# Gating steps ahead of evictions, a chunk's token sums behind the weights, transposes kept whole

## The chip, the cores and the metric

The kernel runs on one core of a Trainium2 chip. The metric is device time in microseconds (us), the median of several executions. Engines are called by the names of the profile: PE (TensorE matmul; PEld is its weight load), DVE (VectorE), ACT (ScalarE), POOL (GpSimd), SP (SyncE, which issues the DMAs).

## The reference

Three parts follow each other; all is float32.

```python
# 1 attention: a pooled branch (mean over groups of 4 positions) and a local one (|i-j| < 4), added
attn_out = out_up + out_local                      # (2, 8, 576, 64)
x = attn_out.transpose(0, 2, 1, 3).reshape(1152, 512)

# 2 mixture of experts over 1152 tokens, D = 512, 8 experts, F = 1024
P = np.exp(x @ w_gate - (x @ w_gate).max())
for _ in range(8):
    P /= P.sum(1, keepdims=True) + 1e-09
    P /= P.sum(0, keepdims=True) + 1e-09
    P *= N / E
for e in range(E):
    out += P[:, e:e + 1] * (np.maximum(x @ w1[e], 0.0) @ w2[e])

# 3 gated stage, F = 1536
return ((out @ w_a) * (out @ w_b)) @ w_out
```

## The kernel before, in words

**Numbers.** Every float32 operand of a large product is split into a rounded high part and a remainder (`xh`, `xl`; `w.hi`, `w.lo`; `gh`, `gl`; `Th`, `Tl`), and each product is three matmuls: high by high, high by low, low by high. A split is a cast on ACT (L132 for weights, L544 for token sums, L680 for transposed tiles) and a subtraction on DVE or POOL (L133, L545, L681).

**Units and chunks.** An expert is two units (halves of F). The 16 expert units are `units[0]` to `units[15]`, the gated stage has six, `glu_g[0]` to `glu_g[5]`. The 1152 tokens are in nine tiles of 128 and two chunks: chunk 0 (tiles 0, 1, 7, 8; 256 columns in each of its halves) and chunk 1 (tiles 2 to 6; 320 columns). The first two units are plain products. All later ones use a scheme with seven products in place of eight: the weights give the operands A11, S2, S1, A12, S3, A22, S4 (S1 to S4 are sums or differences of quarters, `comb`, L236, on POOL; S2, S1, S3 and S4 also have their low parts from POOL), and each takes its token operand from `xh`/`xl` or from the four sums T1 to T4 in `Th`/`Tl`. `g_chunk` issues the seven products of one unit and chunk in that order, each 12 matmuls, and behind each the additions into G tiles (L595) that free the PSUM banks. `phase` puts the second matmuls of the unit and chunk before between them (`o_tile`, one of 128 tokens, 12 matmuls of 512 columns; the results go to `acc` by L464, L466 or L470).

**Token sums.** `combine_x` makes T1 to T4 of one chunk as a list of tasks: four totals (`xh + xl`, L529, two on DVE and two on POOL, or as `tot` says), four differences (L537, DVE) and four splits (L544 on ACT, L545 on DVE or POOL as `low` says).

**What sets the order.** Engines run their instructions in the order in which the program issues them. Side work waits in queues: `wq` (weight preparation), `tq` (token sums), `dq` (decoding of later weights). `pump` runs tasks from them as a planner's clocks `M.pe`, `M.dve`, `M.pool` allow; `force` runs them until a weight that the next product needs is there, `tq` ahead of `wq`. `while tq: run(tq)` empties a queue at once.

**From gating to unit 2.** Once attention is done (`closed`), the gating is a generator that `step` advances by one piece after each product of the first two units (`g_plain`: 4 blocks of unit 1; then three `o_moe` tiles of the first unit): a reduction over experts on DVE, a matmul with ones on PE for the sum over tokens, a reduction and a scaling on DVE, eight times. Then come chunk 0's last sums, chunk 1's sums, and unit 2's products:

```python
        tq.extend(combine_x(1, lambda name: t1[name], (v, g, g, v), (g, g, g, g)))   # chunk 1's sums
        phase(units[2], 0, firsts[1])
```

**From the experts to the gated stage.** The gated stage needs the output transposed: `t_step(tt)` transposes a finished tile of `acc` on PE into a PSUM bank of the pool "o" (two banks, shared with `o_tile`), splits it from there into `xh` (ACT) and `xl` (DVE). The four tiles of chunk 0 are transposed beside the last unit's chunk 1, the five of chunk 1 after it, each one `o_tile` late; the token sums of chunk 0 are queued behind tile 8's step and emptied after three of the five, and the other two `o_tile`s with their steps stand inside `glu_g[0]`'s chunk 0, at places 0, 1 and 2 of its products.

## Time and profile before

| | |
|---|---|
| median of 3 runs | 1185.61 us (1177.13, 1185.61, 1187.04) |
| profiled execution | 1174.93 us, span 1173.2 us |
| mean granted clock of TensorE | 0.974 |
| busy, share of the span | PE 94%, PEld 84%, DVE 71%, ACT 39%, POOL 46% |
| DMA | 84.50 MB, mean 72 GB/s |

The profiled execution is the program run once under the hardware profiler; its span goes from the first to the last instruction. The clock is the mean share of TensorE's full speed that was granted while the program ran. An engine is busy while an instruction of it executes, and the shares are means over stages that differ.

### The profile page before, as it was taken

The numbers are of one execution on the slowest core, as the hardware profiler recorded it, in microseconds if no ns is written. First come the engines' busy times: TensorE is split into PE (matmuls) and PEld (weight loads), VectorE is DVE, ScalarE is ACT, GpSimd is POOL, SyncE is SP. The second block draws the span as 40 slices with busy tenths as digits, with TensorE's granted clock in tenths as the row PEclk, the third lists the DMA queues.
The fourth block names the chain that finished last, engine by engine and source line by source line (L and its number), as shares of the span: only waits on it lengthen the run. The fifth ranks groups of instructions, "written<-read, shape, count | busy, mean of one in ns | idle before, by whom it ended". The sixth has DMA issues, their size and how long they took to land.

```text
span 1173.2 us, 18031 instructions
## 1 busy us (share of the span) xinstructions
PE 1099.5 (94%) x6545; PEld 985.2 (84%) x6545; DVE 838.1 (71%) x1613; ACT 453.2 (39%) x1186; POOL 544.4 (46%) x537
## 2 busy tenths in 40 slices
PE   8898998369999999999999999999999869999998
PEld 6797887358888888988898889889899768999997
DVE  5666455636978898788887987888744677776764
ACT  5654341023444335344444344443443423323221
POOL 3413212333655645555546546554563545555431
PEclk9899999769999999999999999999999989999999
DMA  5342110003313232143232321322211101111102
GB/s 147 99 124 67 34 44 1 0 1 99 115 59 115 91 100 99 56 135 99 72 116 75 116 94 60 119 94 94 88 45 46 37 19 37 55 54 32 42 18 81
DMA packets 79720, 84.50 MB, mean 72 GB/s; under 512 B 34832, under 2 KB 53264, under 8 KB 79632
## 3 DMA queue, kind: packets, MB, share of 16 engines
q1 hardware_dynamic: 79632, 83.36, 22.9%
q8 instruction: 51, 0.84, 0.3%
q14 instruction: 37, 0.30, 0.1%
HBM read 71.54 MB, written 11.80 MB: 71 GB/s over the span
## 4 chain that ended last, share of the span: by engine, by line
PE 76%; DVE 12%; ACT 5%; POOL 3%; issue 2%; DMA 0%; DVEq 0%; SPq 0%; ACTq 0%; POOLq 0%
PE g L60 71%; PE at L60 3%; DVE w L133 3%; ACT w L132 1%; DVE acc L470 1%; DVE G L595 1%; ACT p L832 1%; POOL gl L591 1%; DVE xt L537 1%; ACT G L587 1%; ACT gh L589 1%; POOL p L847 1%; DMA kn<-in_k_dram 0%; DVE dec L338 0%; DVE dec L347 0%
## 5 line engine op out<-in xcount | busy, mean ns | idle before, releaser
L60 PE MATMUL g<-w,gh 128*128 128x512 f32 x1314 | 417.1, 398 | 11.7 <-DVE acc L470 8.1
L60 PE MATMUL g<-xh,w 128*128 128x256 f32 (+2 forms) x1472 | 329.0, 304 | 25.8 <-ACT w L132 23.1
L591 POOL TENSOR_TENSOR gl<-G,gh 128x256 fp32r<-128x256 f32 (+1 forms) x216 | 184.6, 863 | 298.9 <-ACT gh L589 277.3
L60 PEld LDWEIGHTS g<-w,gh 128*128 128x128 f32 x1314 | 237.6, 190 | 57.0 <-DVE acc L470 9.0
L60 PEld LDWEIGHTS g<-xh,w 128*128 128x128 f32 x1472 | 248.3, 190 | 31.9 <-ACT w L132 23.2
L60 PE MATMUL g<-w,gl 128*128 128x512 f32 x657 | 259.3, 395 | 0.0
L60 PE MATMUL g<-Th,w 128*128 128x256 f32 (+1 forms) x960 | 214.7, 300 | 14.4 <-ACT Th L544 4.8
L60 PE MATMUL g<-xl,w 128*128 128x256 f32 (+2 forms) x736 | 222.4, 302 | 0.8 <-POOL xl L905 0.5
L133 DVE TENSOR_TENSOR w<-raw,w 128x512 fp32r<-128x512 f32 x141 | 145.1, 1041 | 105.8 <-ACT w L132 105.8
L595 DVE TENSOR_TENSOR G<-g,G 128x256 f32<-128x256 f32 (+1 forms) x400 | 163.9, 449 | 38.7 <-PE g L60 26.7
L60 PEld LDWEIGHTS g<-Th,w 128*128 128x128 f32 x960 | 162.9, 191 | 21.0 <-ACT Th L544 5.1
L587 ACT ACTIVATE G<-G 128x256 f32<-128x256 f32 (+1 forms) x168 | 74.3, 443 | 244.0 <-DVE G L595 243.0
L60 PEld LDWEIGHTS g<-w,gl 128*128 128x128 f32 x657 | 124.4, 189 | 28.7
L60 PEld LDWEIGHTS g<-xl,w 128*128 128x128 f32 x736 | 139.8, 190 | 5.5 <-POOL xl L905 1.0
L60 PE MATMUL g<-Tl,w 128*128 128x256 f32 (+1 forms) x480 | 142.8, 298 | 0.2 <-DVE Tl L545 0.2
L589 ACT CAST gh<-G 128x256 fp32r<-128x256 f32 (+1 forms) x216 | 93.7, 434 | 109.6 <-DVE G L605 94.2
L132 ACT CAST w<-raw 128x512 fp32r<-128x512 f32 x181 | 107.5, 620 | 23.4 <-POOL raw L236 21.7
L470 DVE SCALAR_TENSOR_TENSOR acc<-g,P,acc 128x512 f32<-128x512 f32 x126 | 93.6, 743 | 23.3 <-PE g L60 22.5
L60 PEld LDWEIGHTS g<-Tl,w 128*128 128x128 f32 x480 | 91.8, 191 | 3.6 <-DVE Tl L545 0.6
L366 POOL TENSOR_TENSOR dec<-dec 128x384 f32<-128x384 f32 x48 | 50.8, 1057 | 77.5 <-DVE dec L363 56.4
L236 POOL TENSOR_TENSOR s<-raw 128x512 f32<-128x512 f32 x40 | 65.2, 1631 | 8.2 <-DMA raw<-in_moe_w_dram 6.7
L133 POOL TENSOR_TENSOR w<-s,w 128x512 fp32r<-128x512 f32 x40 | 59.0, 1474 | 13.9 <-ACT w L132 13.9
(156 smaller groups left out, 1211.9 us busy)
## 6 DMA issues: line engine op xcount, KB each, us to landing
raw<-in_moe_w_dram SPq DMA_DIRECT2D x64, 512.0 KB
w<-dec SPq DMA_DIRECT2D x48, 192.0 KB
dec<-in_moe_w_a_dram SPq DMA_DIRECT2D x16, 384.0 KB
dec<-in_moe_w_b_dram SPq DMA_DIRECT2D x16, 384.0 KB
dec<-in_moe_w_out_dram SPq DMA_DIRECT2D x16, 384.0 KB
raw<-w SPq DMA_DIRECT2D x48, 128.0 KB
raw<-w SPq DMA_DIRECT2D x6, 512.0 KB
vw<-in_v_dram SPq DMA_DIRECT2D x72, 35.0 KB
```

What stands on the lines that cost most here:

```text
L60: nc.tensor.matmul(out=o, lhsT=l, rhs=r, start=start, stop=stop, skip_group_check=not check)
L132: nc.scalar.copy(out=hi, in_=raw)
L133: (low or nc.vector).tensor_tensor(out=lo, in0=raw, in1=hi.bitcast(F32), op=ALU.subtract)
L236: nc.gpsimd.tensor_tensor(out=o(), in0=A(*a), in1=A(*b), op=op)
L366: nc.gpsimd.tensor_tensor(out=tf, in0=tf, in1=mf, op=ALU.add)
L470: nc.vector.scalar_tensor_tensor(out=a, in0=ps, scalar=P[:, tt, u.e:u.e + 1], in1=a, op0=ALU.mult, op1=ALU.add)
L537: nc.vector.tensor_tensor(out=get(o), in0=get(a), in1=get(b), op=ALU.subtract)
L587: nc.scalar.activation(out=src, in_=src, func=AF.Relu)
L589: nc.scalar.copy(out=h, in_=src)
L591: nc.gpsimd.tensor_tensor(out=l, in0=src, in1=h.bitcast(F32), op=ALU.subtract)
L595: nc.vector.tensor_tensor(out=o, in0=bank_, in1=b, op=ALU.add)
L832: nc.scalar.activation(out=p[:, c], in_=sl[:, c * W:(c + 1) * W], func=AF.Exp, bias=nm[:, c:c + 1], scale=1.0, accum_out=rs[:, c:c + 1],)
```

## The change

`mid()` issues a gating step straight after the matmuls of `g_plain` and `o_moe`, ahead of their evictions, in place of `step()` behind them. The first unit's `o_moe` tiles of the last block are evicted by a copy on ACT. `force` runs `wq` alone. Unit 2's A11, A12 and A22 have their low parts from POOL. For the gated stage, `t_step` writes the transposed tile a second time, unsplit, by ACT into `keep` (the freed half of chunk 0's `gh`/`gl` tiles, and two spare tiles); `combine_x` then takes its differences from there, without totals, and splits T2 and T1 ahead of T3 and T4. The nine `t_step`s are issued after the last unit's chunk 1 products: the first chunk-1 `o_tile`, four `t_step`s of chunk 0 in a row, then the other `o_tile`s with one step each; only the last step stands inside `glu_g[0]`.

```diff
     def force(cond):
         while not cond():
-            for q in (tq, wq):
-                if q and (q is tq or not q[0].slot or slot_free() or RING[nring[0] % NSLOT].uses == 0):
-                    run(q)
...
+            run(wq)
...
-        piece("A11", lambda: A(0, 0), (0,), rs[0].ready)
+        piece("A11", lambda: A(0, 0), (0,), rs[0].ready, low)
...
         for j in range(2):
             u.w[f // 2, j].use()
+        mid()
         nc.scalar.activation(out=gh[:, f], in_=ps, func=AF.Relu)
...
+            if u.hf == 0 and closed:
+                nc.scalar.copy(out=a, in_=ps)
+                act(0.65)
+                return
...
         sub("t1", "b12", "t1")
-        total("b21", 2, h0, tot[3])
+        if not tot:
+            sub("b12", "b22", "b12")
+            sub("b22", "b22", "t1")
+            tasks.append(split_t("T2", "b22", low[0]))
+            tasks.append(split_t("T1", "t1", low[3]))
+            sub("b21", "b21", "b22")
+            tasks.append(split_t("T3", "b12", low[1]))
+            tasks.append(split_t("T4", "b21", low[2]))
+            return tasks
...
-        act(0.6)
+        for c in range(2):
+            for h in range(2):
+                a, b = max(HALF[c][h].start, tt * 128), min(HALF[c][h].stop, tt * 128 + 128)
+                if a < b:
+                    o = HALF[c][h].start
+                    nc.scalar.copy(out=keep[c][h][:, :, a - o:b - o], in_=pv[:, :, a - tt * 128:b - tt * 128])
+        act(1.2)
         dve(0.7)
...
-                queue_combined(u)
+                queue_combined(u, nc.gpsimd if u is units[2] else None)
...
+        def mid():
+            if closed:
                 side_step()
...
-        phase(units[last], 1, with_steps(0))
+        phase(units[last], 1, o_tiles(units[last], 0))
...
+        for t, tt in enumerate(TILES[1]):
+            o_tile(units[last], 1, t)
+            if t == 0:
+                for t0 in TILES[0]:
+                    t_step(t0, keep)
+                transposed(0)
+            else:
+                t_step(TILES[1][t - 1], keep)
         while tq:
             run(tq)
...
-        phase(glu_g[0], 0, tiles[3:] + [last_step], True, (0, 1, 2))
+        phase(glu_g[0], 0, [last_step], True, (0,))
```

ACT between the gating and unit 2, before. L435 is `g_plain`'s eviction, L544 the split of a token sum (`b`, `t`: chunk 0; `tgh`, `tgl`: chunk 1), and `w_2750<-raw` the high part of unit 2's A11.

```order
L435 ACTIVATE gh_96<-g_2619 128x384
L544 CAST Th<-b_2515 128x2x256
L544 CAST Th<-b_2487 128x2x256
L544 CAST Th<-b_2713 128x2x256
L544 CAST xh<-t_2466 128x2x256
L544 CAST Th<-tgl_2731 128x2x320
L544 CAST Th<-tgh_2730 128x2x320
L544 CAST Th<-tgl_2731 128x2x320
L544 CAST xh<-tgh_2730 128x2x320
L132 CAST w_2750<-raw 128x512
```

After, with L433 for L435, L464 the new copy to `acc`, `w_2569` A11, `w_2649` S2, `w_2675` S1, `w_2724` A12, and L549 for L544:

```order
L433 ACTIVATE gh_96<-g_2544 128x384
L132 CAST w_2569<-raw 128x512
L433 ACTIVATE gh_96<-g_2572 128x384
L433 ACTIVATE gh_96<-g_2598 128x384
L433 ACTIVATE gh_96<-g_2624 128x384
L132 CAST w_2649<-raw 128x512
L132 CAST w_2675<-raw 128x512
L464 COPY acc_87<-g_2652 128x512
L464 COPY acc_88<-g_2679 128x512
L132 CAST w_2724<-raw 128x512
L464 COPY acc_89<-g_2705 128x512
L549 CAST Th<-b_2515 128x2x256
```

The weights of four operands now stand ahead of chunk 0's splits, and chunk 1's splits are gone from this piece.

POOL from the same place, before. L529 makes totals, L545 low parts of sums, L236 is `comb`, L133 the low part of a weight.

```order
L236 TENSOR_TENSOR s_2542<-raw 128x512
L529 TENSOR_TENSOR b_2713<-xh,xl 128x512
L545 TENSOR_TENSOR Tl<-b_2487,Th 128x2x256
L545 TENSOR_TENSOR Tl<-b_2713,Th 128x2x256
L529 TENSOR_TENSOR tgh_2730<-xh,xl 128x640 x2
L529 TENSOR_TENSOR tgl_2731<-xh,xl 128x640 x2
L545 TENSOR_TENSOR Tl<-tgh_2730,Th 128x2x320
L545 TENSOR_TENSOR Tl<-tgl_2731,Th 128x2x320
L236 TENSOR_TENSOR raw<-raw 128x2x256 x2
L133 TENSOR_TENSOR w_2771<-raw,w_2771 128x512
```

After (L534, L550 and L233 for L529, L545 and L236):

```order
L233 TENSOR_TENSOR s_2542<-raw 128x512
L133 TENSOR_TENSOR w_2569<-raw,w_2569 128x512
L233 TENSOR_TENSOR raw<-raw 128x2x256 x2
L133 TENSOR_TENSOR w_2649<-raw,w_2649 128x512
L133 TENSOR_TENSOR w_2675<-raw,w_2675 128x512
L534 TENSOR_TENSOR b_2702<-xh,xl 128x512
L133 TENSOR_TENSOR w_2724<-raw,w_2724 128x512
L550 TENSOR_TENSOR Tl<-b_2487,Th 128x2x256
L550 TENSOR_TENSOR Tl<-b_2702,Th 128x2x256
L534 TENSOR_TENSOR tgh_2744<-xh,xl 128x640 x2
L534 TENSOR_TENSOR tgl_2745<-xh,xl 128x640
```

A little later on POOL, after: `w_2829` is S3, `gl` the eviction behind the product S3, `s_2870` the `comb` of S4, and `w_2874` A22, whose low part DVE made before.

```order
L133 TENSOR_TENSOR w_2829<-s_2542,w_2829 128x512
L604 TENSOR_TENSOR gl_2749<-G_2435,gh_2747 128x256
L604 TENSOR_TENSOR gl_2749<-G_2436,gh_2747 128x256
L534 TENSOR_TENSOR tgl_2745<-xh,xl 128x640
L233 TENSOR_TENSOR s_2870<-raw 128x512
L133 TENSOR_TENSOR w_2874<-raw,w_2874 128x512
```

Four low parts and two `comb`s of unit 2 now stand ahead of chunk 0's low parts (`Tl`); chunk 1's totals come behind these, in both, and the last of them now has a place between S3 and A22.

ACT at the start of the gated stage, before: L680 is the split of a transposed tile, L587 and L589 the last unit's evictions, `xt` the token sums.

```order
L680 CAST xh<-g_9234 128x4x128 [waits PE_49]
L132 CAST w_9253<-s_9221 128x512 [waits Pool_49]
L587 ACTIVATE G_2433<-G_2433 128x320 [waits DVE_49]
L589 CAST gh_2945<-G_2433 128x320 [waits Activation_49]
L587 ACTIVATE G_2434<-G_2434 128x320 [waits DVE_49]
L589 CAST gh_2945<-G_2434 128x320 [waits Activation_49]
L680 CAST xh<-g_9282 128x4x128 [waits PE_49]
L680 CAST xh<-g_9309 128x4x128 [waits PE_49]
L680 CAST xh<-g_9333 128x4x128 [waits PE_49]
L544 CAST Th<-xt_9290 128x2x256 [waits DVE_49]
```

After, L693 for L680, and L702 the copy to `keep`:

```order
L693 CAST xh<-g_9267 128x4x128 [waits PE_49]
L702 COPY xh<-g_9267 128x4x128 [waits DVE_49]
L693 CAST xh<-g_9275 128x4x128 [waits PE_49]
L702 COPY xh<-g_9275 128x4x128 [waits DVE_49]
L693 CAST xh<-g_9283 128x4x128 [waits PE_49]
L702 COPY xl<-g_9283 128x4x128 [waits DVE_49]
L693 CAST xh<-g_9291 128x4x128 [waits PE_49]
L702 COPY xl<-g_9291 128x4x128 [waits DVE_49]
L693 CAST xh<-g_9315 128x4x128 [waits PE_49]
L702 COPY xt_9248<-g_9315 128x4x128 [waits DVE_49]
```

Each split is followed by a copy of the same bank that waits for DVE, and the splits of five tiles stand in one row.

PE at that place, before: L676 are the transposes of a tile, one group of four behind an `o_tile` of twelve L60 rows.

```order
L676 MATMUL g_9282<-ident,acc_89 128x128 [waits DVE_49]
L676 MATMUL g_9282<-ident,acc_89 128x128 x3
L60 MATMUL g_9291<-w_8858,gh_2945 128x512 [waits DVE_49]
L60 MATMUL g_9291<-w_8858,gh_2945 128x512
L60 MATMUL g_9291<-w_8858,gl_2947 128x512
L60 MATMUL g_9291<-w_8861,gh_2945 128x512 x2
```

After, with L689 for L676:

```order
L689 MATMUL g_9267<-ident,acc_81 128x128 [waits DVE_49]
L689 MATMUL g_9267<-ident,acc_81 128x128 x3
L689 MATMUL g_9275<-ident,acc_82 128x128 [waits DVE_49]
L689 MATMUL g_9275<-ident,acc_82 128x128 x3
L689 MATMUL g_9283<-ident,acc_88 128x128 [waits PE_49,Activation_49]
L689 MATMUL g_9283<-ident,acc_88 128x128 x3
L689 MATMUL g_9291<-ident,acc_89 128x128 [waits PE_49,Activation_49]
L689 MATMUL g_9291<-ident,acc_89 128x128 x3
L60 MATMUL g_9299<-w_8860,gh_2947 128x512 [waits PE_49,Activation_49]
L60 MATMUL g_9299<-w_8860,gh_2947 128x512
```

Four groups of transposes stand in a row behind the chunk's first `o_tile`; from the third on, a group and the next `o_tile` wait for ACT.

## Rows read from the trace of the kernel before

**Rows 1.** Waits of PE from the gating's end to unit 2's first chunk (217.4 to 275).
```profile
PE g L60 <- ACT w L132: 25.2, 4, 23.1
PE g L60 <- DVE w L133: 3.6, 2, 2.0
PE g L60 <- POOL w L133: 1.4, 2, 0.8
```

**Rows 2.** Timeline of PE, same stretch: start, us, instruction, idle before.
```profile
217.49 0.34 PE L60 MATMUL g<-P,ones 128*128 128x72 f32 x2
240.88 0.58 PE L60 MATMUL g<-xh,w 128*128 128x256 f32 x1 [23.05 <-ACT w L132]
...
254.44 0.28 PE L60 MATMUL g<-xh,w 128*128 128x256 f32 x1
...
257.19 0.28 PE L60 MATMUL g<-xh,w 128*128 128x256 f32 x1
...
261.07 0.62 PE L60 MATMUL g<-w,gh 128*128 128x512 f32 x2
```

**Rows 3.** Windows, same stretch: us, busy of PE, PEld, DVE, ACT, POOL, clock, DMA.
```profile
240.00:254.00 14.00, 9.55 (x35) 8.02 (x36) 4.16 (x4) 3.13 (x7) 6.88 (x5) 0.55 0.00 1
266.00:270.00 4.00, 3.69 (x14) 3.44 (x15) 1.10 (x3) 1.48 (x4) 0.73 (x1) 0.57 0.74 259
```

**Rows 4.** Timeline of DVE after the gating.
```profile
219.40 0.69 DVE L537 TENSOR_TENSOR t<-b,t 128x512 f32<-128x512 f32 x1 [0.17 <-issue]
...
222.35 0.69 DVE L545 TENSOR_TENSOR Tl<-b,Th 128x512 fp32r<-128x512 f32 x1 [0.73 <-ACT Th L544]
222.96 1.77 DVE L537 TENSOR_TENSOR b<-b,b 128x512 f32<-128x512 f32 x1
```

**Rows 5.** Timeline of POOL after the gating.
```profile
222.91 1.26 POOL L545 TENSOR_TENSOR Tl<-b,Th 128x512 fp32r<-128x512 f32 x1 [32.96 <-ACT Th L544]
...
230.10 3.60 POOL L529 TENSOR_TENSOR tgl<-xh,xl 128x640 f32<-128x640 f32 x2
...
258.47 1.27 POOL L133 TENSOR_TENSOR w<-s,w 128x512 fp32r<-128x512 f32 x1 [8.76 <-ACT w L132]
263.00 1.49 POOL L591 TENSOR_TENSOR gl<-G,gh 128x256 fp32r<-128x256 f32 x2 [3.25 <-ACT gh L589]
264.44 1.26 POOL L236 TENSOR_TENSOR s<-raw 128x512 f32<-128x512 f32 x1
```

**Rows 6.** Waits of PE during the gating (185 to 217.4).
```profile
PE g L60 <- DVE acc L464: 1.2, 2, 0.6
PE g L60 <- DVE P L957: 1.1, 4, 0.4
```

**Rows 7.** Waits of PE around the gated stage's start (905 to 990).
```profile
PE g L60 <- DVE acc L470: 7.1, 4, 3.2
PE g L60 <- ACT Th L544: 4.8, 1, 4.8
PE g L60 <- DVE G L595: 2.1, 2, 1.7
```

**Rows 8.** Timeline of PE there: two `o_tile`s and their transposes.
```profile
933.72 0.71 PE L60 MATMUL g<-w,gh 128*128 128x512 f32 x2 [2.25 <-DVE acc L470]
...
936.55 0.60 PE L676 MATMUL g<-ident,acc 128*128 128x128 f32 x4
...
946.36 1.22 PE L60 MATMUL g<-w,gh 128*128 128x512 f32 x2 [3.20 <-DVE acc L470]
...
951.65 0.94 PE L676 MATMUL g<-ident,acc 128*128 128x128 f32 x4
```

**Rows 9.** Window there, columns as in rows 3.
```profile
968.00:972.00 4.00, 3.07 (x10) 2.72 (x11) 2.92 (x2) 1.64 (x3) 1.56 (x1) 0.50 0.00 0
```

**Rows 10.** Timelines of ACT there: one split of a tile from PSUM.
```profile
931.51 0.59 ACT L680 CAST xh<-g 128x512 fp32r<-128x512 f32 x1 [3.28 <-PE g L676]
```

**Rows 11.** Timeline of DVE there: the other split of the same bank.
```profile
933.50 0.67 DVE L681 TENSOR_TENSOR xl<-g,xh 128x512 fp32r<-128x512 f32 x1
```

More of the change, by code (lines that the diff above doesn't have):

```diff
@@ L171, in force @@
         while not cond():
-            for q in (tq, wq):
-                if q and (q is tq or not q[0].slot or slot_free() or RING[nring[0] % NSLOT].uses == 0):
-                    run(q)
-                    break
-            else:
+            if not (wq and (not wq[0].slot or slot_free() or RING[nring[0] % NSLOT].uses == 0)):
                 raise RuntimeError("nothing left to prepare")
+            run(wq)
     class Raw:
@@ L222, in queue_plain, with queue_combined @@
                 wq.append(Task(piece, 0.68, ready=rs[j].ready, slot=True))
-    def queue_combined(u):
+    def queue_combined(u, low=None):
         u.s = {}
@@ L265, in queue_combined @@
         piece("S1", lambda: A(1, 0), (0,), None, pl)
-        piece("A12", lambda: A(0, 1), (1,), None)
+        piece("A12", lambda: A(0, 1), (1,), None, low)
         piece("S3", lambda: tmp["s3"], (), None, pl)
         comb("S4", (0, 1), (0, 0), ALU.subtract, s3, (0, 1), None)
-        piece("A22", lambda: A(1, 1), (1,), None)
+        piece("A22", lambda: A(1, 1), (1,), None, low)
         piece("S4", lambda: tmp["s3"], (), after("S4"), pl)
@@ L456, in o_mm, with o_moe @@
         return ps
-    def o_moe(u, gh, gl, t, tt):
+    def o_moe(u, gh, gl, t, tt, mid=None):
         ps = o_mm(u, gh, gl, t)
+        if mid:
+            mid()
         pump()
@@ L548, in split_t @@
             return Task(fn, *cost(e))
-        total("t1", 0, h0, tot[0])
-        total("b12", 0, h1, tot[1])
-        total("b22", 2, h1, tot[2])
+        if tot:
+            for x, e in zip((("t1", 0, h0), ("b12", 0, h1), ("b22", 2, h1), ("b21", 2, h0)), tot):
+                total(*x, e)
         sub("t1", "b12", "t1")
-        total("b21", 2, h0, tot[3])
+        if not tot:
[7 more added lines that the diff above has]
+            return tasks
         sub("b12", "b22", "b12")
@@ L972, in gating @@
             )
-            dve(0.95)
+            dve(0.85)
     def side():
@@ L1171, in attn_moe_glu_kernel @@
                 lambda n=n, t=t, b=b: o_moe(
-                    units[n], *([G[n][:, f] for f in range(4)] for G in GP), t, b * per + t)
+                    units[n], *([G[n][:, f] for f in range(4)] for G in GP), t, b * per + t, mid)
                 for t in range(per)
@@ L1191, in attn_moe_glu_kernel @@
         for x, G in (("h", GH), ("l", GL)):
-            t = g0p.tile([128, 4, 512], F32R, name=f"g{x}_0")
-            G.append([t[:, f] for f in range(4)])
+            t = [g0p.tile([128, 2, 512], F32R, tag=f"g{x}_0{n}", name=f"g{x}_0{n}") for n in range(2)]
+            G.append([t[f // 2][:, f % 2] for f in range(4)])
         def o_tile(u, c, t):
@@ L1253, in attn_moe_glu_kernel, with transposed, last_step @@
         phase(units[last], 0, o_tiles(units[last - 1], 1))
-        phase(units[last], 1, with_steps(0))
+        phase(units[last], 1, o_tiles(units[last], 0))
         t4p = ctx.enter_context(tc.tile_pool(name="t4p", bufs=1, side="right"))
         G4 = t4p.tile([128, 320], F32, name="G4")
-        tiles = with_steps(1)
-        for t in tiles[:3]:
-            t()
+        keep = [
+            [g0p.tile([128, KT, 256], F32, tag=f"g{x}_01", name=f"x{x}") for x in "hl"],
+            [spare_tile(i, F32, f"xt{i}")[:, 0:KT * 320].rearrange("p (k n) -> p k n", k=KT) for i in range(2)],
+        ]
+        def transposed(c):
+            x0, x1 = keep[c]
+            where = {"t1": x0[:, 0:2], "b12": x1[:, 0:2], "b22": x1[:, 2:4], "b21": x0[:, 2:4]}
+            tq.extend(combine_x(c, lambda name: where[name], (v, g, g, v), None))
+        for t, tt in enumerate(TILES[1]):
[4 more added lines that the diff above has]
+                transposed(0)
+            else:
+                t_step(TILES[1][t - 1], keep)
         while tq:
             run(tq)
-        phase(glu_g[0], 0, tiles[3:] + [last_step], True, (0, 1, 2))
+        def last_step():
+            t_step(TILES[1][-1], keep)
+            transposed(1)
+        phase(glu_g[0], 0, [last_step], True, (0,))
         while tq:
```

36 lines of the change are left out of this document (9 added, 27 removed).

## Prediction

> **What bounds the kernel now.** The share of busy time by engine names PE, at 94%; a bound at that share is beaten only where PE stands still or runs slowly, so I looked for those places in the list of PE's waits, and left out attention, which the diff doesn't touch. Two stretches remain. In the first, between the gating and unit 2, PE waits 25.2 us for weight casts on ACT, 3.6 us for DVE's low parts and 1.4 us for POOL's, 30.2 us together [rows 1]. One wait makes most of it: the last gating matmul is at 217.49, unit 2's first product at 240.88 after 23.05 us of nothing [rows 2]. Here the reader is to see what ACT is held by: in the order before, the cast of A11 stands behind all eight splits of token sums, chunk 1's among them, which the first seven products don't need. The second stretch is the change from the experts to the gated stage, with 7.1 us of waits for evictions, 4.8 us for a token sum and 2.1 us for additions to G tiles [rows 7], 14.0 us together. After each long wait PE also runs at the lower of its two levels, 1.2 in place of 2.4 GHz: the granted clock is 0.55 from 240 to 254, 0.57 from 266 to 270 [rows 3], and 0.50 from 968 to 972 [rows 9].
>
> **Gating steps ahead of evictions.** During the gating PE waits 1.1 us for the scaled P and 1.2 us for the eviction of a tile by DVE [rows 6]. In the new order the gating's DVE pieces stand ahead of the evictions, and the three tile copies are ACT's, which has little to do there. Both waits can go: 2.3 us. Against it stands POOL's new work: by the order four low parts and two combinations come under the gating, where POOL had one total and one combination. What that does to DVE is seen once in the trace: a difference of 512 columns took 0.69 us alone and 1.77 us when it started 0.05 us behind a POOL subtraction of 1.26 us [rows 4, 5]; it ended after POOL's plus its own time. A gating step has two DVE instructions with both inputs in SBUF. With six POOL instructions of about 1.27 us more, the cost lies between nothing (all fall beside other DVE work) and six full waits, 7.6 us; I take 1.5 us, one or two hits, since only two of about nine DVE instructions of a step are exposed. The gating's end so moves by about 1 us, to near 216.7.
>
> The Trainium skill's page "SBUF — State Buffer", section "Who interferes with whom", says the same more strictly: a DVE instruction with two SBUF inputs and a GpSimd instruction that reads SBUF share a port pair that is an exclusive lock, held for the whole instruction. The pair of rows just named agrees with it. It speaks against putting POOL's work here.
>
> **Chunk 1's sums behind unit 2's weights.** A11's weights are cast and split under the gating (ACT and POOL rows of the order), so A11 follows the last gating matmul at once. What is late next, product by product:
> - S2 needs T2. Before, DVE's first difference came 1.9 us behind the last gating matmul with a tile's copy ahead of it, 0.6 us by the waits that such a copy made [rows 6], so it is now 1.3 us behind. From it to the end of T2's low part took 3.6 us (219.40 to 223.04) [rows 2, 4], so T2 is whole after 4.9 us. PE has the gating matmul and A11, 1.6 us (24 matmuls of this size start between 254.44 and 257.3, so 12 take 1.44 us [rows 2]). Wait: 3.0 us, taking off what S2's first high parts cover.
> - S1 and A12 have their weights already. Nothing.
> - S3's cast and POOL part stand as near to the product as before. Besides the long one, the waits for casts are 2.1 us in three, those for POOL 1.4 us in two [rows 1]; I take one of each at the long side, with ACT and POOL busier: 2.3 us.
> - A22's low part is now POOL's and stands behind a pair of evictions, a total and S4's combination. The pair starts 1.9 us behind the product S3 (263.00 on POOL; PE goes on to the tile at 261.07 [rows 2, 5]) and takes 1.49 us; a total is half of 3.60 us, the combination 1.26 us, a part itself 1.27 us (258.47) [rows 5]: 7.7 us. PE's cover is one tile of 2.83 us (933.72 to 936.55 [rows 8]) and the product's first two matmuls, 0.35 us. Wait: 4.5 us, where DVE's wait was 1.6 us, the shorter of two [rows 1]. This is the one edit here that costs.
> - S4: 0.2 us.
>
> That is 10.0 us in place of 30.2 us. The slow clock before cost about half of the PE time under it: about 4 us of the 9.55 us busy from 240 to 254 (the last two are quick again), and 1.8 us of the 3.69 us from 266 to 270 [rows 3]; I put A22's longer wait down for 2 us again, so 4 us are gained. Chunk 1's sums move under unit 2's first chunk, where DVE and POOL waited for PE; by the order they are done before the second chunk asks for them. **Stretch one: 20.2 + 4 + 2.3 - 1.5 = 25 us**, between 19 (all six POOL waits, 7.6 in place of 1.5) and 29 (none of them, and A22 no later than before).
>
> **Transposes kept unsplit.** Eight totals go, four on DVE and four on POOL; nine tiles are copied once more, in ten ACT copies. In PSUM one tile is one bank, the pool has two, and by the order the copy waits for DVE's reading of the bank and the next but one user waits for the copy. So a step is a chain on ACT: cast 0.59 us [rows 10], DVE's part 0.67 us [rows 11], a copy of the cast's shape which I take at the cast's 0.59 us, with handing over about 1.95 us. The copy is not in the trace of before: its price has the cast as the nearest row, from nothing to twice that. Four steps in a row take 7.8 us and PE's share is at most 4 x 0.60 us [rows 8], and since the groups overlap I take 1.4 us. The third and fourth transposes and the next tile wait: the tile starts once the third step's copy is done, about 6.4 us on, so PE idles 5.0 us, and I charge 2.5 us for the low clock behind it, as behind 946.36, where a tile took 5.29 us (to 951.65) in place of 2.83 us [rows 8]. The later steps stand one to a tile: 1.95 us under 2.83 us. I allow 0.8 us for an eviction there and 2.4 us for one that comes behind the token sums and weights on DVE. Loss: 10.7 us.
>
> What it replaces: 14.0 us of waits, 2.8 us of low clock at the tile of 946.36 and its transposes (0.94 us in place of 0.60) [rows 8] and about 1.5 us of the 3.07 us busy from 968 to 972 [rows 9], 18.3 us. The 4.8 us wait for T2 of chunk 1 [rows 7] goes, because the differences start straight from the copies and T2 is split first: walked through in the same way, it is whole about 2 us before PE asks. **Stretch two: 7.6 us, of which I count 7**; between 2 (the low clock stays for another tile and an eviction waits as long as the 3.2 us there is now) and 11 (no low clock). With copies at nothing or double, a step is 1.4 or 2.5 us and the first idle 3.3 or 6.8 us, inside these bounds.
>
> Elsewhere PE's order and the DMAs stay; the tiles' buffers cost nothing that I can see.
>
> **Sum.** 25 + 7 = 32 us from the profiled 1174.93 us: 1143 us. The profiled execution is 0.9% under the median of the three runs, two of which lie near 1186 us and one near 1177 us; by the median it is 1153 us. I say 1150 us. Within 1% is about what this measurement can't tell from no change.
>
> **The rivals.**
> - *POOL holds DVE up under the gating.* For it: the one pair of rows above, and six instructions put there. Against: most gating instructions have one SBUF input or a PSUM one. Stretch one 19 us, total 26: 1159 us by the median. It is also what the page's lock gives at its strictest.
> - *The copies eat the second stretch.* Four steps in a row are a longer stall than any there is now in that stretch. If PE stays at 1.2 GHz until the chunk's tiles are through, 5 us more are lost and evictions pile up: the stretch gives nothing, total 25: 1160 us.
> - *The first stall moves on and doesn't go* (the change doesn't do what it says): S2, S3 and A22 all wait on DVE and POOL, with the clock low throughout as from 240 to 254. At 1.2 GHz seven products and three tiles, 18.6 us, take 18.6 us more in place of the 2 us above; stretch one gives about 8, total 15: 1170 us. Against: now the clock is up again from 254.
> - *Slower:* the low level holds in the gated stage. The mechanism is the row of copies: PE starved for 6 us, then fed so thinly that the clock stays at 1.2 GHz. Each us of full-speed work then costs one more us; the first stretch's 25 us are used up, and 12 more to show, after 37 us of work, that is, all of `glu_g[0]`'s chunk 0 and most of its chunk 1. Total: 1197 us and more. Against: of the tiles there now, only the one of 946.36 runs at the low clock.
> - *Better:* the lock costs nothing, clock and evictions hold at both places: 29 + 11 = 40 us, 1145 us by the median.
>
> **How the numbers follow.** Forecast 0.5; POOL's hold 0.15; the copies 0.15; the stall that moves on 0.07; slower 0.03; better 0.10. Most of the first stall is removed in all but two of them, so faster by over 1% has 0.93, within 1% 0.04, slower 0.03. The range: its low end is a gain of 38 us on the profiled level, 1137 us; its high end a gain of 21 us on the median, 1165 us. That leaves out the stall that moves on, the slower case, and half of the better one.
>
> **What would show it.** In the new profile: no wait near 23 us behind the last gating matmul; waits of about 3, 2 and 4.5 us ahead of S2, S3 and A22, the last on POOL; unit 2's first chunk ends 24 to 30 us sooner; gating steps that are no longer than before. At the gated stage: a wait of PE of about 5 us in the row of transposes, on ACT's L702; no wait for L549 ahead of chunk 1. I am wrong if A11 itself waits, if gating steps stretch by a us or more, or if the clock stays low past the tile behind the transposes.

## The result and the profile after

The changed kernel takes 1162.39 us in the median of 20 runs, the kernel before 1182.41 us in 20 runs: a ratio of 0.9831 (95% interval 0.9805 to 0.9857), 20.0 us less. That is inside the predicted range and faster by more than 1%, as forecast, with 20 us in place of the 32 us of the sum. The profiled execution of the changed kernel has a span of 1167.1 us, just 6 us under the profiled one of before. To see where the time went I cut both traces at seven starts in PE's timeline: the first product of unit 0 behind attention's last transposes, the last matmul with ones, the first row of matmuls of 320 columns of unit 2, of unit 3, of the last expert unit, of gated unit 0 and of gated unit 1. The differences, in us:

| stretch | before | after | change | forecast |
|---|---|---|---|---|
| attention | 185.35 | 199.74 | +14.4 | 0 |
| gating | 32.14 | 34.59 | +2.5 | -0.8 |
| unit 2's chunk 0 | 56.23 | 34.15 | -22.1 | -24.2 |
| unit 2's chunk 1, unit 3's chunk 0 | 51.28 | 54.13 | +2.9 | 0 |
| to the last unit's chunk 1 | 572.97 | 574.64 | +1.7 | 0 |
| last unit's chunk 1, gated unit 0's chunk 0 | 64.15 | 67.13 | +3.0 | -7 for both |
| gated unit 0's chunk 1, gated unit 1's chunk 0 | 43.22 | 35.24 | -8.0 | |
| the rest | 163.86 | 163.86 | 0.0 | 0 |
| from the gating on | 983.85 | 963.74 | -20.1 | -32 |

From the gating on the traces differ by 20.1 us, which is the difference of the medians; a second profile of the changed kernel (after_again, below) gives 16.1 us. The 14.4 us in attention are of this one execution. In windows of the profile after (us, busy of PE, PEld, DVE, ACT and POOL, clock, DMA) PE is busy all the time from 40 to 70, and slow:

```profile
30.00:40.00 10.00, 6.80 (x40) 5.83 (x39) 5.64 (x19) 5.17 (x24) 6.13 (x13) 0.79 0.40 88
40.00:52.00 12.00, 12.00 (x61) 11.02 (x60) 6.46 (x21) 5.65 (x24) 2.33 (x3) 0.50 0.13 28
52.00:60.00 8.00, 8.00 (x41) 7.51 (x41) 4.21 (x16) 4.49 (x19) 1.90 (x3) 0.50 0.32 91
60.00:70.00 10.00, 10.00 (x50) 9.23 (x50) 5.13 (x16) 4.34 (x17) 3.31 (x4) 0.50 0.63 154
```

The same in the profile before:

```profile
30.00:40.00 10.00, 8.86 (x49) 7.92 (x50) 4.89 (x18) 4.92 (x24) 5.93 (x12) 0.66 0.39 90
40.00:50.00 10.00, 9.18 (x82) 8.31 (x81) 7.55 (x27) 6.75 (x29) 3.63 (x5) 1.00 0.14 32
```

Both executions lose the full clock between 30 and 40; one gets it back at once, the other stays at 1.2 GHz for some 33 us with PE never idle. No engine has another order of instructions there. Taking from the medians what the profiles show from the gating on, and the 5.7 and 5.6 us that an execution's time has beyond the stretches (1174.93 - 185.35 - 983.85, and 1169.11 - 199.74 - 963.74), leaves 192.8 us for attention before and 193.0 us after, so the change has no part in it that the medians would show. The granted clock of all executions agrees. What the lower level costs an execution is, by estimate, at most (1 - clock) times its span: in the median 38 us in 37 executions of the kernel before and 29 us in 20 of the changed one. In the two profiles it is 30.5 and 38.5 us, of which 6.8 and 23.9 us lie in attention and 23.7 and 14.6 us behind it. A typical execution of either kernel so loses some 14 us in attention; the two profiles lie on either side of that.

The first stretch, in the waits of PE from the last gating matmul to unit 2's chunk 1 (us in total, times, longest), answers to [rows 1]:

```profile
PE g L60 <- POOL w L133: 5.3, 3, 4.0
PE g L60 <- ACT Th L549: 2.6, 1, 2.6
PE g L60 <- ACT w L132: 1.0, 1, 1.0
PE g L60 <- DVE Tl L550: 0.3, 1, 0.3
```

9.2 us in place of 30.2 us. PE's timeline (start, us, instruction, idle before) shows where, and answers to [rows 2]:

```profile
227.21 0.41 PE L60 MATMUL g<-P,ones 128*128 128x72 f32 x2 [1.93 <-DVE P L976]
...
234.33 0.34 PE L60 MATMUL g<-P,ones 128*128 128x72 f32 x2
234.47 0.36 PE L60 MATMUL g<-xh,w 128*128 128x256 f32 x1
...
238.74 0.39 PE L60 MATMUL g<-Th,w 128*128 128x256 f32 x1 [2.58 <-ACT Th L549]
...
249.21 0.38 PE L60 MATMUL g<-Th,w 128*128 128x256 f32 x1 [0.98 <-ACT w L132]
...
250.56 0.51 PE L60 MATMUL g<-Th,w 128*128 128x256 f32 x2 [0.84 <-POOL w L133]
...
260.60 0.50 PE L60 MATMUL g<-Th,w 128*128 128x256 f32 x2 [4.04 <-POOL w L133]
```

A11 follows the last gating matmul at once. S2 waits for T2 (2.58 us), S3 for its cast and its low part (0.98, 0.84), A22 for POOL (4.04). The window rows that answer to [rows 3] show a low clock behind the waits of S2, S3 and A22. The first row belongs to none of them: it is the start of the gating, which ran at 1.2 GHz in this execution.

```profile
199.70:203.00 3.30, 3.26 (x10) 3.26 (x11) 1.20 (x2) 0.00 (x0) 3.30 (x3) 0.50 0.00 0
241.00:244.00 3.00, 3.00 (x9) 2.32 (x9) 1.79 (x4) 1.68 (x4) 2.16 (x2) 0.50 0.02 5
251.00:254.00 3.00, 3.00 (x13) 2.71 (x12) 1.62 (x5) 0.41 (x1) 0.00 (x0) 0.50 0.00 0
260.00:264.00 4.00, 3.40 (x14) 3.11 (x15) 1.73 (x3) 1.64 (x4) 1.28 (x2) 0.64 0.82 254
```

What the low clock costs in the stretch is read from PE's busy time over all of it, before, after, and in the kernel best (below), which did the same work at the full clock:

```profile
217.49:273.72 56.23, 26.01 (x124) 21.90 (x123) 27.02 (x34) 13.50 (x28) 24.87 (x19) 0.70 0.07 21
234.33:268.48 34.15, 24.94 (x125) 21.27 (x125) 17.54 (x29) 9.86 (x22) 17.69 (x14) 0.85 0.13 39
223.10:252.20 29.10, 20.57 (x124) 17.33 (x123) 18.95 (x29) 9.74 (x22) 17.00 (x13) 1.00 0.17 56
```

So PE's work there takes 20.6 us at the full clock; the low clock added 5.4 us before and 4.4 us after.

At the gated stage's start, PE's waits (897 to 977) answer to [rows 7]; the 4.8 us wait for T2 of chunk 1 is gone, and waits for the copies L702 are there:

```profile
PE g L60 <- DVE acc L474: 3.1, 3, 2.3
PE g L60 <- DVE G L608: 2.8, 1, 2.8
PE g L689 <- ACT xh L702: 2.7, 2, 1.9
PE g L60 <- ACT xl L702: 0.7, 1, 0.7
```

PE's timeline of the four transposes in a row and the tile behind them answers to [rows 8]:

```profile
923.36 0.60 PE L689 MATMUL g<-ident,acc 128*128 128x128 f32 x4
924.37 0.66 PE L689 MATMUL g<-ident,acc 128*128 128x128 f32 x4 [0.41 <-DVE acc L474]
926.97 1.12 PE L689 MATMUL g<-ident,acc 128*128 128x128 f32 x4 [1.95 <-ACT xh L702]
928.80 1.12 PE L689 MATMUL g<-ident,acc 128*128 128x128 f32 x4 [0.71 <-ACT xh L702]
930.63 1.22 PE L60 MATMUL g<-w,gh 128*128 128x512 f32 x2 [0.71 <-ACT xl L702]
...
934.85 0.60 PE L689 MATMUL g<-ident,acc 128*128 128x128 f32 x4
```

The tile took 4.2 us, partly on the low clock.

### The profile page after: what moved, and what is told of

Same layout as the page of the kernel before. It is cut to its first block, busy times and chain, and to the rows that moved or that the text cites. A ratio compares the mean times of both kernels' runs of the same rounds, so it can differ in the third digit from the quotient of the medians.

```text
span 1167.1 us, 18045 instructions
## 1 busy us (share of the span) xinstructions
PE 1114.9 (96%) x6545; PEld 1000.2 (86%) x6545; DVE 823.5 (71%) x1603; ACT 459.5 (39%) x1199; POOL 539.4 (46%) x536
## 4 chain that ended last, share of the span: by engine, by line
PE 37%; DVE 23%; ACT 9%; issue 4%; POOL 3%; DMA 2%; DVEq 0%; ACTq 0%; POOLq 0%; SPq 0%
PE g L60 37%; DVE w L133 6%; DVE acc L474 4%; DVE G L608 3%; ACT w L132 3%; ACT G L600 2%; POOL gl L604 2%; ACT gh L602 2%; DVE dec L335 2%; DVE dec L331 1%; DVE dec L344 1%; DVE gl L594 1%; DVE dec L356 1%; DVE dec L348 1%; DMA dec<-in_moe_w_b_dram 1%
## 5 line engine op out<-in xcount | busy, mean ns | idle before, releaser
L60 PE MATMUL g<-w,gh 128*128 128x512 f32 x1314 | 418.7, 400 | 10.0 <-DVE acc L474 5.0
L60 PE MATMUL g<-xh,w 128*128 128x256 f32 (+2 forms) x1472 | 330.2, 305 | 0.8 <-POOL w L133 0.4
L60 PEld LDWEIGHTS g<-w,gh 128*128 128x128 f32 x1314 | 238.5, 190 | 56.1 <-DVE acc L474 8.2
L60 PE MATMUL g<-w,gl 128*128 128x512 f32 x657 | 260.2, 396 | 0.0
L60 PEld LDWEIGHTS g<-xh,w 128*128 128x128 f32 x1472 | 250.4, 191 | 6.4 <-DVE G L608 0.9
L60 PE MATMUL g<-Th,w 128*128 128x256 f32 (+1 forms) x960 | 212.7, 297 | 14.3 <-DVE G L608 5.7
L60 PE MATMUL g<-xl,w 128*128 128x256 f32 (+2 forms) x736 | 223.3, 303 | 0.2 <-POOL xl L924 0.2
L133 DVE TENSOR_TENSOR w<-raw,w 128x512 fp32r<-128x512 f32 x138 | 141.6, 1037 | 110.3 <-ACT w L132 110.3
L60 PEld LDWEIGHTS g<-Th,w 128*128 128x128 f32 x960 | 161.5, 189 | 20.4 <-DVE G L608 5.8
L60 PEld LDWEIGHTS g<-w,gl 128*128 128x128 f32 x657 | 125.0, 190 | 28.9
L60 PEld LDWEIGHTS g<-xl,w 128*128 128x128 f32 x736 | 140.9, 191 | 4.4 <-POOL xl L924 0.5
L60 PE MATMUL g<-Tl,w 128*128 128x256 f32 (+1 forms) x480 | 142.1, 296 | 0.3 <-DVE Tl L550 0.3
L60 PEld LDWEIGHTS g<-Tl,w 128*128 128x128 f32 x480 | 91.0, 190 | 3.7 <-DVE Tl L550 0.5
L133 POOL TENSOR_TENSOR w<-raw,w 128x512 fp32r<-128x512 f32 x43 | 58.3, 1363 | 31.8 <-ACT w L132 31.8
L233 POOL TENSOR_TENSOR s<-raw 128x512 f32<-128x512 f32 x40 | 66.1, 1653 | 5.0 <-DMA raw<-in_moe_w_dram 4.6
```

Source lines behind the costliest of these rows:

```text
L60: nc.tensor.matmul(out=o, lhsT=l, rhs=r, start=start, stop=stop, skip_group_check=not check)
L133: (low or nc.vector).tensor_tensor(out=lo, in0=raw, in1=hi.bitcast(F32), op=ALU.subtract)
L233: nc.gpsimd.tensor_tensor(out=o(), in0=A(*a), in1=A(*b), op=op)
```

## The experiments

Times of a few per mille are hard to tell apart in medians whose runs spread over 10 us and more, so the stretches of the profiles carry most of the argument. All kernels' stretches, in us, cut as above:

| kernel | gating | unit 2 c0 | unit 2 c1, 3 c0 | to last c1 | to gated 0 c1 | to gated 1 c1 | from the gating on |
|---|---|---|---|---|---|---|---|
| before | 32.14 | 56.23 | 51.28 | 572.97 | 64.15 | 43.22 | 983.85 |
| changed | 34.59 | 34.15 | 54.13 | 574.64 | 67.13 | 35.24 | 963.74 |
| order_only | 32.09 | 43.40 | 62.88 | 575.25 | 64.44 | 43.52 | 985.46 |
| no_order | 34.43 | 40.38 | 49.71 | 575.08 | 67.11 | 35.18 | 965.75 |
| gated_only | 32.94 | 56.47 | 51.46 | 574.78 | 69.49 | 35.21 | 984.21 |
| low_none | 29.14 | 43.27 | 59.92 | 573.93 | 67.16 | 35.20 | 972.48 |
| psum_scalers | 31.06 | 34.67 | 53.27 | 573.26 | 66.24 | 35.74 | 958.33 |
| no_mid | 39.07 | 34.04 | 53.24 | 574.21 | 67.14 | 35.19 | 966.75 |
| a22_dve | 36.01 | 30.24 | 55.72 | 573.34 | 69.48 | 35.18 | 963.83 |
| keep_first | 35.94 | 33.45 | 54.06 | 573.92 | 64.76 | 35.42 | 961.41 |
| best | 31.18 | 29.17 | 55.20 | 575.21 | 64.79 | 35.51 | 955.15 |
| after_again | 37.42 | 34.47 | 53.96 | 575.95 | 66.45 | 35.65 | 967.77 |

The long middle column, in which nothing differs by intent, goes from 573.0 to 576.0 us: 2 us there, and so its +1.7 us above, are no effect. The two profiles of the changed kernel differ by 2.8 us in the gating.

In the gating, the windows of the profile tell two things apart: how long PE stood still, and the clock. PE stood still for 2.98 us in before and order_only (2.39 in gated_only), 0.65 in low_none, 4.24 to 4.26 in changed, no_order, a22_dve, keep_first and after_again, 1.03 and 1.02 in psum_scalers and best, and 7.04 in no_mid. The mean clock was 1.00 in before, order_only and low_none, 0.95 in changed, no_order, gated_only, psum_scalers and best, 0.91 in a22_dve, keep_first and no_mid, and 0.87 in after_again. In the five kernels with the changed gating as it stands, PE stands still equally long; that their gating takes 34.4 to 37.4 us is the clock.

**The queue order alone (order_only).** Before, with one edit:

```diff
-            for q in (tq, wq):
-                if q and (q is tq or not q[0].slot or slot_free() or RING[nring[0] % NSLOT].uses == 0):
-                    run(q)
-                    break
-            else:
+            if not (wq and (not wq[0].slot or slot_free() or RING[nring[0] % NSLOT].uses == 0)):
                 raise RuntimeError("nothing left to prepare")
+            run(wq)
```

> The kernel before with one edit: preparing a weight that the next product needs no longer runs the token sums first. If the queue order carries the gain by itself, the stretch from the last gating matmul to unit 2's second chunk falls from 56.2 us by nearly all of the 22 us that the whole change gained there, to 35 us. If it needs the weights prepared under the gating as well (POOL making their low parts), A11's cast still comes behind chunk 0's four splits, about 8.5 us behind the last gating matmul in place of 23.4, and the stretch is 41 to 44 us. Gating 32.1 us and the gated stage's start (64.2 + 43.2 us) as before; the time some 12 to 15 us under before in the second case.

Measured: ratio 0.998 (0.9946 to 1.0014), no gain where I expected 12 to 15 us. Unit 2's chunk 0 took 43.4 us, the second of the two cases; but what it gained, 12.8 us, came back in the next stretch, 62.9 us in place of 51.3. One row of PE's timeline shows it, the first T product of unit 2's chunk 1:

```profile
269.06 0.64 PE L60 MATMUL g<-Th,w 128*128 128x320 f32 x1 [6.04 <-ACT Th L541]
```

The stall had moved on to where chunk 1's sums are needed. This is the thought of my third rival, a stall that moves on and doesn't go, though at another place than the S2, S3 and A22 that it named: what the sums' place saves ahead of chunk 0 they ask for ahead of chunk 1, as long as unit 2's chunk 0 is too short to hide them and its own weights are still to be made.

**All but the queue order (no_order).** The changed kernel with the old loop in `force` (the diff above, backwards).

> The changed kernel with the old rule: a weight that is needed runs the token sums first. A11 to A12 are prepared under the gating all the same, so the stall moves to S3, whose low part stands behind chunk 1's totals and splits on POOL. By durations (totals 7.1 us, two differences 4 us, splits about 3 us, behind chunk 0's two low parts) it is ready some 22 us behind the last gating matmul where PE asks after 13: a wait of 8 us, and A22's 4 us go. The stretch is 38 to 40 us in place of 34.2 if that is right; 34 us if the order doesn't matter once the weights are made early; 50 us or more if the order alone made the gain.

Measured: ratio 0.9839 (0.9743 to 0.9936). Chunk 0 took 40.4 us with a wait of 9.5 us at S3, a little over the 40 and the 8 us that I had worked out:

```profile
244.67 0.58 PE L60 MATMUL g<-Th,w 128*128 128x256 f32 x1 [9.52 <-ACT w L132]
```

It gave 4.4 us of the 6.2 us back in the next stretch (49.7 us), where the sums were then ready. From the gating on 965.75 us, 2.0 us over the changed kernel's first profile and 2.0 us under its second: the queue order is worth about nothing once the weights are made early.

**The gated stage's part alone (gated_only).** Before with the hunks of `combine_x`, `t_step` and the order of the gated stage's start, nothing else.

> The kernel before with the gated stage's part alone (transposes kept whole, no totals, the transposes moved). Theory from the two traces: the stretch from the last expert unit's chunk 1 to the gated unit 0's chunk 1 gets 3 us longer (64.2 to 67 us), since four transposes in a row wait on ACT's copies, and the next 8 us shorter (43.2 to 35.2 us), since T2 is ready: 5 us in all. Rival: the part owes its gain to the state in which the first part leaves the engines, and gives under 2 us alone. All stretches ahead as before (gating 32.1, then 56.2 us).

Measured: ratio 0.9951 (0.9916 to 0.9987), and in the profile 64.15 to 69.49 us, then 43.22 to 35.21 us: 2.7 us gained. In the eight profiles that carry the part as it stands the two stretches together take 102 us (six times) or 104.7 us (twice; 107.4 before), so it gives 2.7 to 5.4 us, and it does so without the first part: the rival falls. The two profiles of the longer level (gated_only and a22_dve) have one more stretch of 3.4 us at the clock of 0.50 there; what brings it on stays open. From the gating on, gated_only's profile shows no gain (984.2 against 983.9 us), because the stretches that the edit doesn't touch took 3.0 us more; its median is 6.2 us lower.

**Low parts on DVE again (low_none).**

```diff
-                queue_combined(u, nc.gpsimd if u is units[2] else None)
+                queue_combined(u)
```

> The changed kernel with unit 2's A11, A12 and A22 low parts on DVE again. It tells what made the gating longer (34.6 us in place of 32.1). If POOL's six instructions hold DVE up there, they move behind the gating (the planner finds no room for A11 on DVE) and the gating takes 29.5 to 31 us. If the gating steps ahead of the evictions are what costs, it stays at 34 us or more. Behind it, A11's cast comes after chunk 0's splits: the stretch is 40 to 44 us in place of 34.2, and the whole 4 to 8 us slower than the changed kernel.

Measured: ratio 0.9890 (0.9827 to 0.9953). The gating takes 29.1 us, 5.5 us less than in the changed kernel, and PE no longer waits for P there. Of the 5.5 us, 3.6 us are PE standing still (4.24 to 0.65 us). Most of the rest is the low clock at the start of the changed kernel's gating: its first step took 10.7 us, and 9.1 us here and in no_order, which has the same work on POOL and had the full clock there. Chunk 0 takes 43.3 us and the next stretch 59.9 us, nearly as in order_only: it is the making of the weights under the gating, which POOL's low parts allow, that removes the stall. Without it the time from the gating on is 972.5 us, 8.7 us more than in the changed kernel's first profile (4.7 us more than in its second).

**The reciprocals in PSUM (psum_scalers).**

```diff
-        rt = const.tile([128, NT], F32, name="rt")
-        ct = const.tile([128, E], F32, name="ct")
+        pc = ps3_
         for it in range(NITER):
+            rt = pc[:, 128:128 + NT]
...
             mm(pc[:, 0:NT * E], ones, Pf, True, True)
+            ct = pc[:, 144:144 + E]
```

> The changed kernel with one edit: the gating's two vectors of reciprocals (9 and 8 columns) lie in the PSUM bank of the step's matmul instead of SBUF, so that the two scalings of P have one SBUF input each. POOL's work, the order and the count of instructions stay. If POOL holds up just the DVE instructions with two SBUF inputs, the gating falls from 34.6 us to 29 to 30.5 us (29.1 where POOL had nothing to do there), with all its steps under 3.1 us but the last two; the rest unchanged, so some 5 us in all. Rival: POOL slows any DVE work, or the steps wait for something else: gating still over 33 us.

Measured: ratio 0.9757 (0.9716 to 0.9797); gating 31.1 us, 3.5 us less than the changed kernel's first profile and 6.4 us less than its second, just over the 29 to 30.5 us expected; no step behind the first over 3.7 us. DVE's timeline of the changed kernel in the step in which PE waited longest, POOL's beside it:

```profile
221.25 0.17 DVE L974 TENSOR_SCALAR rt<-rt 128x9 f32<-128x9 f32 x1
...
223.25 1.35 DVE L988 SCALAR_TENSOR_TENSOR P<-P,ct 128x72 f32<-128x72 f32 x1
224.63 0.23 DVE L973 TENSOR_REDUCE rt<-P 128x9 f32<-128x72 f32 x1
224.90 0.88 DVE L974 TENSOR_SCALAR rt<-rt 128x9 f32<-128x9 f32 x1
225.81 0.22 DVE L975 RECIPROCAL rt<-rt 128x9 f32<-128x9 f32 x1
226.06 1.00 DVE L976 TENSOR_TENSOR P<-P,rt 128x72 f32<-128x72 f32 x1
```

```profile
223.22 2.53 POOL L133 TENSOR_TENSOR w<-raw,w 128x512 fp32r<-128x512 f32 x2 [5.33 <-ACT w L132]
225.71 1.26 POOL L534 TENSOR_TENSOR b<-xh,xl 128x512 f32<-128x512 f32 x1
```

The same lines in psum_scalers, with POOL at the same work:

```profile
214.10 0.23 DVE L989 SCALAR_TENSOR_TENSOR P<-P,g 128x72 f32<-128x72 f32 x1
214.36 0.24 DVE L973 TENSOR_REDUCE g<-P 128x9 f32<-128x72 f32 x1
214.63 0.17 DVE L974 TENSOR_SCALAR g<-g 128x9 f32<-128x9 f32 x1
214.84 0.23 DVE L975 RECIPROCAL g<-g 128x9 f32<-128x9 f32 x1
215.10 0.23 DVE L976 TENSOR_TENSOR P<-P,g 128x72 f32<-128x72 f32 x1
```

```profile
214.01 2.54 POOL L133 TENSOR_TENSOR w<-raw,w 128x512 fp32r<-128x512 f32 x2 [3.73 <-ACT w L132]
```

The scalings L988 and L976 took 1.35 and 1.00 us beside POOL, 0.23 us without; and so did L974, which adds a constant to nine columns, 0.88 us in place of 0.17. The reduction L973 and the reciprocal L975 between them took their 0.23 and 0.22 us. With the vectors in PSUM none of these instructions is held, and PE stands still for 1.03 us in the gating in place of 4.24. Of the 1.9 us that are left over low_none's gating, some 1.5 us are the low clock at its start (0.95 over the stretch). So POOL holds up certain DVE instructions that have all operands in SBUF, not DVE as such: the rival falls.

**Gating steps behind the evictions (no_mid).** The changed kernel without `mid`, the copy on ACT and the planner's cost.

> The changed kernel without the gating steps ahead of the evictions (they stand behind, as before, and DVE copies the first unit's tiles); the weights are still made under the gating. If what the step order gives (32.1 to 29.1 us with POOL idle) adds to POOL's hold, the gating takes 37 to 38 us; if the hold falls into the waits that the old order has anyway, 34 to 35.5 us.

Measured in one execution: 1172.29 us; gating 39.1 us, over both cases, PE waiting 6.2 us for P. With POOL idle the step order gave 3.0 us (32.1 to 29.1), with POOL at work it gives 1.7 to 4.5 us (against the changed kernel's two profiles). In PE's standing still, which the clock doesn't blur, it is 2.3 us (2.98 to 0.65) and 2.8 us (7.04 to 4.24): step order and hold add, and the hold doesn't fall into waits that are there anyway. What lies over the 37 to 38 us is low clock.

**A22's low part on DVE (a22_dve).**

```diff
-        piece("A22", lambda: A(1, 1), (1,), None, low)
+        piece("A22", lambda: A(1, 1), (1,), None)
```

> The changed kernel with A22's low part alone on DVE again. By my reading the wait of 4.0 us ahead of A22 is POOL's queue (two evictions, a total, a combination ahead of it), so it falls to 1.6 us or less, and the low clock behind it costs less: 31 to 32.5 us in place of 34.2 us from the last gating matmul to unit 2's second chunk. Rival: DVE has chunk 1's first difference in the same place, which waits for the same total, and A22 still waits 3 us or more; the stretch stays at 33.5 us or above.

Measured in one execution: 1166.83 us; the stretch takes 30.2 us, 3.9 us less, a little more than expected. PE's timeline at A22 and at S4:

```profile
256.21 0.50 PE L60 MATMUL g<-Th,w 128*128 128x256 f32 x2 [1.83 <-DVE w L133]
...
262.00 0.51 PE L60 MATMUL g<-xh,w 128*128 128x256 f32 x2 [1.33 <-POOL w L133]
```

1.83 us in place of 4.04 us; S4 waits 1.33 us in place of 0.42 us. In all, PE stood still for 8.1 us in the stretch in place of 9.2, so only 1.1 of the 3.9 us are waits. The rest is PE's busy time, 22.0 us in place of 24.9, at a clock of 0.94 in place of 0.85: no low clock came behind the waits of S3 and A22 here (1.00 from 245 to 262). The next stretch is 1.6 us longer, so 2.3 us stay; from the gating on this profile has the changed kernel's time, as its gating and its gated stage were longer.

**The unsplit copy ahead of DVE's reading (keep_first).** In `t_step` the copies to `keep` stand ahead of the subtraction:

```diff
         nc.scalar.copy(out=xh[:, :, sl], in_=pv)
-        nc.vector.tensor_tensor(
-            out=xl[:, :, sl], in0=pv, in1=xh[:, :, sl].bitcast(F32), op=ALU.subtract
-        )
         for c in range(2):
...
+        nc.vector.tensor_tensor(
+            out=xl[:, :, sl], in0=pv, in1=xh[:, :, sl].bitcast(F32), op=ALU.subtract
+        )
```

> The changed kernel with the unsplit copy of a transposed tile issued ahead of DVE's reading of the bank instead of behind it, so that ACT's two readings follow each other and its next step needn't wait for DVE. A step then holds ACT 1.2 us in place of 1.8; with two banks, four steps take about 5 us in place of 7.3. PE's waits for the copies (3.4 us there) fall to about 1 us and the stretch to the gated unit 0's second chunk from 67.1 to 64 us; the rest unchanged. Rival: the chain is in the bank, not on ACT, since cast, copy and DVE's part follow each other in it either way: 66.5 us or more.

Measured: ratio 0.9760 (0.9721 to 0.9799); the stretch takes 64.8 us, 2.4 us less. ACT's timeline in the changed kernel, first two of the four steps (the cast row answers to [rows 10]):

```profile
924.99 0.58 ACT L693 CAST xh<-g 128x512 fp32r<-128x512 f32 x1
926.33 0.58 ACT L702 COPY xh<-g 128x512 f32<-128x512 f32 x1 [0.76 <-DVE xl L694]
926.81 0.59 ACT L693 CAST xh<-g 128x512 fp32r<-128x512 f32 x1
928.16 0.58 ACT L702 COPY xh<-g 128x512 f32<-128x512 f32 x1 [0.76 <-DVE xl L694]
```

And in keep_first:

```profile
915.48 0.58 ACT L693 CAST xh<-g 128x512 fp32r<-128x512 f32 x1
915.95 0.59 ACT L699 COPY xh<-g 128x512 f32<-128x512 f32 x1
916.43 0.60 ACT L693 CAST xh<-g 128x512 fp32r<-128x512 f32 x1
916.91 0.61 ACT L699 COPY xh<-g 128x512 f32<-128x512 f32 x1
```

The 0.76 us that ACT spent waiting for DVE in each step are gone. PE still waits 2.6 us there in all (in place of 3.4; I expected about 1), now for DVE's reading: two banks are the bound behind ACT, so a part of the rival holds.

**The three together (best), and the changed kernel again (after_again).**

> The changed kernel with the three edits that helped alone: reciprocals in PSUM, A22's low part on DVE, the unsplit copy ahead of DVE's reading. If the gains lie in different places and add, the gating takes 31 us, the stretch to unit 2's second chunk 30 to 31, the one to the gated unit 0's second chunk 64.5 to 65: from the gating on 955 to 957 us in place of 963.7, and the median 7 to 9 us under the changed kernel's. If they take from each other (A22 on DVE comes earlier into a DVE that is busier), under 4 us.

> The changed kernel once more, beside the one above on the same chip. From the gating on 963 to 966 us as in the first profile, 20 us under the kernel before (983.9), while attention, whose order is the same in both, may take anything from 185 to 200 us: then the 14 us by which it was longer in the first profile are chance and no part of the change. If attention again takes over 195 us here while the kernel before stays near 185, the change does something to it after all.

Measured on one chip: best 1154.91 us, ratio 0.9738 (0.9690 to 0.9786); changed kernel again 1160.79 us, ratio 0.9796 (0.9753 to 0.9839). From the gating on best has 955.15 us, in each stretch about what its edit gave alone; 8.6 us under the changed kernel's first profile, 12.6 us under its second, 5.9 us in the medians, under the 7 to 9 us expected, and the intervals overlap. In the stretch of unit 2's chunk 0, best's waits were 8.5 us and the clock 1.00 (row above), so a part of its gain there is clock and not waits. The changed kernel again took 967.8 us from the gating on, over the 963 to 966 us expected, with the clock at 0.87 in its gating. Its attention took 196.9 us, over the 195 us that I had set as the sign of an effect. In the profiles attention took 185.4 to 185.8 us in the three kernels with the gating of before, and 186.8 (no_order) to 200.2 us in the nine others, though all twelve have the same order there. Against an effect stand the medians, which leave the same 193 us to both kernels, and the granted clock of all executions, which leaves the same 14 us of low clock. I take it for chance.

## Why the prediction came out as it did

The forecast held in direction and range; its sum was 12 us too high, mainly in four terms. The range held with some luck: its upper end was laid as a gain of 21 us on three runs with a median of 1185.6 us, and the gain was 20.0 us on 20 runs whose median was 3.2 us lower. Stretch one gave 19.6 us, which is the 19 us of the rival "POOL holds DVE up" and not the 25 us of the forecast. Two of the signs that the prediction had set spoke against it: two gating steps became longer by over a us (2.8 to 4.0 us and 3.1 to 5.1 us), and unit 2's first chunk ended 19.6 us sooner and not 24 to 30.

- **A11 at once, S2, S3, A22, S4: right.** Forecast 3.0, 2.3, 4.5 and 0.2 us of waits, 10.0 in all; measured 2.9, 1.8, 4.0 and 0.4, 9.2 in all. The A22 wait was POOL's queue (a22_dve).
- **The low clock in that stretch: mis-sized by 2.9 us.** I had 4 us gained and one low stretch of 2 us left. There were three, behind the waits of S2, S3 and A22, and they cost 4.4 us where the low clock cost 5.4 us before: 1.1 us gained. The step that failed is that a low clock would come behind A22's wait alone. Nor is it a fixed price: best had nearly the same waits (8.5 us in place of 9.2) and the full clock. The 18.6 us of full-speed work in my third rival is low; it is 20.6 us.
- **The gating: mis-sized by 3.3 us.** The step order takes the 2.3 us of PE's standing still that I forecast (2.98 to 0.65, low_none against before). POOL's hold costs 3.6 us of it (0.65 to 4.24) where I took 1.5 us of a range up to 7.6. PE's busy time is another 1.2 us longer than before (29.2 to 30.4), with the low clock at the gating's start, for which I had no term; gated_only, with the gating of before, has it at the same place, so it isn't shown to come from the change. The step that failed is that only two of about nine DVE instructions of a step are exposed: the additions of a constant are held too, so it is up to four of nine, all on the chain that PE waits for. Seven instructions were held in all, for 5.2 us, of which 3.6 us reached PE. The rule of the page "SBUF — State Buffer" of the Trainium skill, in its section "Who interferes with whom", has both kinds: instructions with two SBUF inputs, and tensor_scalar among those that can take both ports. The rows agree with it; the 3.6 us lie between my 1.5 and the 7.6 us of its strictest reading.
- **Chunk 1's sums under unit 2's chunk 0: not free.** I had "done before the second chunk asks for them", which is right, but the next stretch is 2.9 us longer: waits of 1.0 us for a cast and 1.4 us for a low part, where there was one of 1.0 us, and a low clock behind them. The waits stand ahead of matmuls of `w` and `gh`, unit 2's second layer, whose weights are prepared behind the sums. That order_only gives back 11.6 of its 12.8 us in the same place shows how little room there is.
- **Stretch two: 5.0 us in place of 7**, the mechanism as worked out: four steps on ACT at 1.83 us each, the tile behind them at 930.63, 7.3 us behind the first transposes (923.36), on the low clock (4.2 us in place of 2.8), and no wait for T2. The waits for copies were 3.4 us in place of 5.0; evictions (3.5 us) and additions to G tiles made up for it. For the additions I had put nothing, as if the 2.1 us of before went, and they took 2.8 us.

What carries the gain, by the experiments: no_order has all of it but 2 us (by the changed kernel's first profile), so the queue order is not what carries it. low_none, without the early weights, has 11.4 us: 3.0 us from the shorter gating, 5.0 us from the gated stage, and 4.3 us in which the two stretches of unit 2 together are shorter than before (103.2 against 107.5 us), less 1 us in the middle column. The early weights give the other 8.7 us (4.7 us by the second profile), after POOL's hold has taken 3.6 us of what they bring.

## What to carry to other kernels

Moving a task behind the one that waits now moves the stall to whoever needs the task next; look there before counting the gain, and read the granted clock behind each wait that is left: nearly the same waits came with 4.4 us of low clock here and with none in best. Work handed to POOL beside a DVE chain is priced by what DVE's instructions on that chain read: a vector in PSUM instead of SBUF took 3.2 of the 3.6 us away here. Where two engines read one PSUM bank in turn, put the readings of one engine behind each other.
